# HGRN2 attention with a bilinear feed-forward: block 1 half in product triples, the weights' conversion in the list scheduler

## Chip, cores and metric

The kernel runs on one core of a Trainium2 chip. The metric is the device time of one execution in microseconds (us); the time of the kernel before is the median of three runs.

## What is computed

```
f = sigmoid(f_logit)                                   # (4 batches, 8 heads, 768 steps, 48)
state[t] = f[t][:, None] * state[t-1] + outer(k[t], v[t])
y[t]     = q[t] @ state[t]
x   = y of all heads side by side                      # 3072 tokens x 384
out = ((x @ w_a) * (x @ w_b)) @ w_out                  # w_a, w_b: 384 x 1536; w_out: 1536 x 384
```

All in float32 on the chip; the three weight matrices arrive as 64-bit floats.

## The kernel before

**Attention.** The scan is computed in 16 units of 2 x 2 heads and 384 steps, with running products of f (DVE scans), masked scores of 64 x 64 tokens, and states carried from chunk to chunk. Each unit needs loads of f, k, q and v (SP queue), a front on ACT, POOL and DVE (`front_parts`), matmuls (`core_parts`), and five stores of y into `xT` over SP (L554). Two units make the x of one block of 384 tokens; there are eight blocks.

**Feed-forward, up.** For a block, x @ w_b and x @ w_a are made in 12 column tiles of 128. In the direct form (`up_steps`, L598) a tile takes six matmuls of 384 columns, three into each of two PSUM banks. There are four banks, so a tile's two banks are those of the tile two before it. `product` (L618, L620) lets ACT copy the b half to SBUF and DVE multiply it with the a half; this frees the banks. Blocks 0 and 1 use the direct form for all 12 tiles. Blocks 2 to 7 use `up_triples` (L720): three column tiles k of a group j together, three row blocks of the weights and two halves of the tokens are multiplied with fifteen products instead of eighteen, from sums of weights (`combine_w_ba`) and sums of x (`combine_x`), 4 groups a block. The sums of weights overwrite parts of w_ba, so they can only be finished when no direct tile needs w_ba any more.

**Feed-forward, down.** `down` (L822) multiplies two token groups of 128 by w_out with seven products instead of eight, from sums of w_out (`combine_w_out`).

**Weights.** 20 pieces (`weight_pieces`: 14 of w_b and w_a by column tiles, 6 of w_out), 768 KB each (four are 384 KB), are loaded by SP (L258) and converted to float32 by `from_double` in steps: ACT makes the exponent word (L58) and the low word (L59), POOL bounds the exponent (L60), ACT makes the sign in two instructions (L62, L63), DVE shifts (L68) and adds (L73). A piece is loaded into one of four places of `raw`; pieces 4 and 5 lie in `groups`, where later the products of block 1 lie. Three pieces at a time have room for their intermediate words (`thirds`, `bits`).

**The order.** Every engine works through its instructions in the order in which the code emits them. Up to tile 5 of block 0 the order is written by hand. Then comes a loop over `ups`: block 0's tiles 6 and 7, then tiles of block 1 and block 0 in turn, and it converts the weights tile by tile as `needed` asks for them (`convert`, `begin`, `end`). The last tiles and all that follows are a list `main` of steps with costs; a list scheduler puts the steps of six `Line`s beside it (sums of w_out, sums of x, the attention's core and front, its loads, sums of w_ba). `fill` emits a line's step when by the planner's costs it can start within a beat (653 ns, one product on PE) and does not make a step of `main` late against its due beat, with a margin of 500 ns (`delays`). The sums of w_ba use 11 adding DMAs from the POOL queue (L630), six writes on ACT (L633) and four additions on DVE (L1256).

Of the kernel before, what the change touches and what calls it, by code (L numbers as in the profile page):

```python
# [12 lines left out]
FP32 = mybir.dt.float32  # L13
# [129 lines left out]
def by_quotients(ctx, tc, q, k, f_logit, v, moe_w_a, moe_w_b, moe_w_out, out, ident, weights, bad, ps_f):  # L143
# [53 lines left out]
    raw_places = itertools.cycle([raws4[:, PIECE * i:PIECE * i + PIECE] for i in range(4)])  # L197
# [43 lines left out]
    EARLY = (4, 5)  # L241
# [3 lines left out]
    def load_weights(n=1):  # L245
        for _ in range(n):
            if len(raws) == len(todo):
                return
            dst, src, (k, m) = todo[len(raws)]
            raw = dst  # L250
            if src.dtype != FP32:

                if len(raws) in EARLY:
                    raw = groups[:, EARLY.index(len(raws))].bitcast(mybir.dt.uint64)
                else:
                    raw = next(raw_places)
                raw = raw[:, 0:k * m].rearrange("p (k m) -> p k m", k=k)
            nc.sync.dma_start(out=raw, in_=src)  # L258
            raws.append(raw)
# [16 lines left out]
    def end(n):  # L276

        while ended[0] < min(n, len(todo)):
            begin(ended[0] + 1)
            next(going[ended[0]], None)  # L280
            ended[0] += 1
            if ended[0] > 2 and ended[0] - 1 not in EARLY:
                load_weights()

    def convert(n):
        while ended[0] < min(n, len(todo)):
            end(ended[0] + 1)
            begin(ended[0] + 2)
# [6 lines left out]
    firsts = groups[:, len(EARLY)].rearrange("p (u n s) -> p u n s", u=NQ, n=2)  # L295
# [6 lines left out]
    def front_parts(u):  # L302
# [38 lines left out]
        first = ((ACT, 930, opposite), (ACT, 750, sigmoid))  # L341
# [270 lines left out]
    def product():  # L612

        if not factors:
            return
        blk, ft, ps = factors.pop(0)
        b_sb = next(b_copies)
        nc.scalar.copy(b_sb, ps["b"][:, 0:BLK])  # L618
        a, b = (x.rearrange("p (g t) -> p g t", g=NTG) for x in (ps["a"][:, 0:BLK], b_sb))
        nc.vector.tensor_tensor(products(blk)[:, :, ft], a, b, ALU.mult)  # L620
        give_back(ps.values())
# [13 lines left out]
    def w_sums(steps, width):  # L635

        for to, x, what in steps:
            if what in (1, -1):
                yield ACT, width, 0, write, to, x, what
            elif what == "+":  # L640
                yield POOL, 1300, 0, add_by_dma, to, x
            else:
                yield DVE, width + 200, 0, nc.vector.tensor_tensor, to, x, *what
# [8 lines left out]
    def combine_w_out():  # L652
# [6 lines left out]
            (t1, b12, (b11, ALU.subtract)), (t2, b22, (t1, ALU.subtract)),  # L659
            (t4, b21, (t2, ALU.subtract)), (b12, b22, (b12, ALU.subtract)),  # L660
        ), 1070)

    def combine_w_ba():
# [10 lines left out]
        )  # L674
        return w_sums((
            (s[1], a12, 1), (s[4], a33, -1), (s[5], a11, -1), (s[1], a22, "+"), (s[4], a31, "+"), (s[5], a31, "+"),
            (s[3], a22, 1), (s[2], a12, 1), (s[0], a21, 1), (s[1], a23, "+"), (s[4], a21, "+"), (s[5], a32, "+"),
            (s[3], a23, "+"), (s[2], a22, "+"), (s[0], a32, "+"), (s[3], a32, "+"), (s[2], a21, "+"),
        ), 1000), w_sums((
            (a31, a11, (a31, ALU.subtract)), (a31, a31, (a33, ALU.add)),  # L680
            (a22, s[1], (a31, ALU.subtract)), (a22, a22, (a13, ALU.add)),
# [32 lines left out]
    def up_triples(blk):  # L714
# [28 lines left out]
        for j in range(NJ3):  # L743
# [9 lines left out]
            first, second = (x.rearrange("p (g n t) -> p g n t", g=2, n=2) for x in pairs)  # L753
# [15 lines left out]
            yield copy(3, first[:, :, 1], u)  # L769
# [3 lines left out]
            yield copy(3, first[:, :, 0], v)  # L773
            yield on(DVE, 870, 0, add_steps, c[:, :, 1:3, 1], c[:, :, 1:3, 1], first, copied=True)
# [5 lines left out]
            yield copy(3, second[:, :, 1], v)  # L780
# [5 lines left out]
            yield copy(2 if j == NJ3 - 1 else 3, second[:, :, 0], v)  # L786
            yield times(u, "u5", j)
            yield add(3, 2, 0, u)
            yield on(DVE, 870, 0, add_steps, c[:, :, 0], c[:, :, 0], second, copied=True)
# [178 lines left out]
    with tc.manual_schedule():  # L968
# [98 lines left out]
        end(3)  # L1067
        load_unit(3, "v")
        end(4)
        turn(2)  # L1070
# [21 lines left out]
        load_weights(2)  # L1092
# [6 lines left out]
        end(7)  # L1099
        mask(3)  # L1100
# [5 lines left out]
        end(8)  # L1106
        carried(3)
        product()
        begin(10)
        end(9)  # L1110
        up(0, 5)
# [5 lines left out]
        ups = [(0, 6), (0, 7)]  # L1117
        for i in range(8, NFT):
            ups += [(1, i - 8), (0, i)]
        ups += [(1, i) for i in range(NFT - 8, NFT)]  # L1120
        alone = len(todo) - 7
        for n, (blk, i) in enumerate(ups[0:alone]):
            convert(needed(i))
            up(blk, i)
            end(8 + n)
            product()
            begin(ended[0] + 2)
            if 2 < n < 2 + 2 * NSET and n % 2:
                load_unit(NSET + n // 2, "kqv" if n == 3 else "fkqv")


        w_out_sums, (w_before, w_over) = list(combine_w_out()), combine_w_ba()
        main, beside, behind, ending = [], {}, {}, []
        for blk, i in ups[alone:]:
            main.extend(up_steps(blk, i))
            main.append(on(DVE, 480, 2, product))
        behind[0] = behind[1] = len(main)
        ahead = 4
        for blk in range(NBLK):
            if blk >= 2:  # L1140
                beside[len(main)] = "x", blk
                main.extend(up_triples(blk))
# [4 lines left out]
            if blk == 1:  # L1147
                pairs = (((0, 1), (0, 2)), *pairs)
            for two in pairs if blk else ():
# [4 lines left out]
                beside = {n + (n > at): x for n, x in beside.items()}  # L1154
# [4 lines left out]
                behind.setdefault("down", len(main))  # L1159
# [15 lines left out]
        for_out, for_x, core, fore, loads, for_ba = lines = [Line() for _ in range(6)]  # L1175
        marks = {"out": for_out.extend(w_out_sums)}
        for_ba.extend(w_before)
        marks["ba"] = for_ba.extend(w_over, past=behind[1])
        stores = {}
        for s in range(2 * NQ, NU + 1):  # L1180
            if s < NU:
                loaded = ()
                if s - NSET in stores:
                    at = stores[s - NSET]
                    loaded = (loads.extend([(SP, ISSUE, 6000, do) for do in loads_of(s)], needs=(at,)),)
                ready = fore.extend(
                    [(e, load, 0, *do) for part in front_parts(s) for e, load, *do in part], needs=loaded
# [10 lines left out]
            if s > 2 * NQ and s % NQ == 0:  # L1198
                blk = s // NQ - 1
                one_by_one = combine_x(blk)  # L1200
                marks["x", blk] = for_x.extend(
                    [(e, load, 0, next, one_by_one) for e, load in X_STEPS],
                    needs=(stores[s - 1],),
                    past=behind[blk - 1] if blk > 2 else behind["down"],
                )

        LATENCY, MARGIN = 200, 500
        now, free_at, done = 0, [0] * 5, 0
# [11 lines left out]
        def delays(engine, start, load):  # L1220
# [17 lines left out]
            for ready, cost, due in later:  # L1238
# [3 lines left out]
                if with_it + MARGIN > max(starts.get(due, 1 << 30), without + MARGIN):  # L1242
# [3 lines left out]
        def emit(line, start):  # L1246
            nonlocal now
# [4 lines left out]
            else:  # L1252
                free_at[engine] = start + load
            line.ends.append(start + load + after)
# [11 lines left out]
        def fill():  # L1266
            more = True
            while more:
                more = False
                for line in lines:  # L1270
# [15 lines left out]
        for done, (engine, load, due, do, *args) in enumerate(main):  # L1286
            if done in beside:
                emit_until(*marks[beside[done]])
                if beside[done] == ("x", 2):
                    emit_until(*marks["ba"])  # L1290
# [363 lines left out]
```

## Time and profile before

| | |
|---|---|
| median of 3 runs | 596.82 us (596.09 to 597.02) |
| the profiled execution | 596.65 us |
| its span | 594.9 us |
| PE's granted clock, mean | 0.997 |
| direct matmuls L598, 128x384, 288 records | busy 95.6 us |
| adding DMAs L630, 11 | 8.5 us median to landing |
| ACT waits for PE's triples (sums, L1301) | 68.2 us |

The span runs from the first instruction to the last. PE is TensorE, DVE VectorE, ACT ScalarE, POOL GpSimd, SP SyncE, which only issues DMAs here. A float32 matmul leaves two records. The busy time of a group counts overlapping records once, so one product is priced by the distance of the next, not by its own duration. An engine's idle time is put down to the instruction that released it.

### The profile page before, as it was taken

Reading aid. Unit: us, or ns where it says so; the run is one execution under the profiler, and the core shown is the slowest. Engines: PE = TensorE matmul, PEld = TensorE weight load, DVE = VectorE, ACT = ScalarE, POOL = GpSimd, SP = SyncE. Lnnn points to the kernel's source line nnn. Section 1 sums busy time; section 2 is a strip of 40 time slices with the busy share of each in tenths; the row PEclk is TensorE's granted clock in tenths of the full one; section 3 lists DMA queues with packets and bytes.
Section 4 is the critical chain, followed back from the end, with each engine's and each line's share of the span. In section 5 each row is a group of like instructions: output and inputs, shape, how many; then the busy total and the mean of one; then the engine's idle time right before and its main releaser. Section 6 shows DMA issues by size and latency. Waiting matters only on the chain.

```text
span 594.9 us, 13948 instructions
## 1 busy us (share of the span) xinstructions
PE 573.2 (96%) x5802; PEld 513.2 (86%) x5802; DVE 411.9 (69%) x786; ACT 268.9 (45%) x507; POOL 77.6 (13%) x71
## 2 busy tenths in 40 slices
PE   3899999999999999999999999999999999999996
PEld 1655655567999999999999999999999999999996
DVE  6899445599978678958895678837785265745741
ACT  6589959743122464245521344326431335135300
POOL 6254525355000000000000000000000000000000
PEclk9899999999999999999999999999999999999999
DMA  8696698099552440043005400041001100000000
GB/s 205 192 261 211 220 264 257 0 154 186 115 141 66 115 99 4 15 120 95 2 1 127 115 15 1 2 112 36 3 1 47 48 1 0 2 28 1 0 29 33
DMA packets 33273, 49.43 MB, mean 83 GB/s; under 512 B 3952, under 2 KB 24976, under 8 KB 33200
## 3 DMA queue, kind: packets, MB, share of 16 engines
q1 hardware_dynamic: 30000, 42.38, 25.8%
q0 software_dynamic: 3056, 5.92, 5.8%
q8 instruction: 47, 0.77, 0.5%
q14 instruction: 26, 0.21, 0.1%
q10 hardware_dynamic: 144, 0.15, 0.1%
HBM read 33.23 MB, written 4.72 MB: 64 GB/s over the span
## 4 chain that ended last, share of the span: by engine, by line
PE 84%; DVE 11%; issue 2%; ACT 1%; DMA 1%; SPq 0%; DVEq 0%; ACTq 0%
PE ps_f L720 35%; PE ps_f L822 28%; PE ps_f L598 13%; PE ps_y L489 2%; DVE inv L335 2%; PE ps_y L515 2%; PE ps_x L392 2%; PE ps_x L440 1%; PE ps_x L416 1%; DVE sums L712 1%; DVE f_in L322 1%; DVE groups L712 1%; DVE st L469 1%; DVE q_in L339 1%; DVE spare L335 1%
## 5 line engine op out<-in xcount | busy, mean ns | idle before, releaser
L598 PE MATMUL ps_f<-xT,w_ba 128*128 128x384 f32 x288 | 95.6, 489 | 0.9 <-DMA xT<-y 0.7
L1301 ACT COPY sums<-ps_f 128x384 f32<-128x384 f32 x120 | 57.4, 480 | 75.9 <-PE ps_f L720 68.2
L598 PEld LDWEIGHTS ps_f<-xT,w_ba 128*128 128x128 f32 x288 | 54.0, 190 | 37.5 <-issue 1.6
L1301 ACT COPY groups<-ps_f 128x384 f32<-128x384 f32 x120 | 57.7, 481 | 62.9 <-PE ps_f L720 39.9
L720 PE MATMUL ps_f<-xT,w_ba 128*128 128x192 f32 x384 | 78.5, 327 | 0.0
L720 PEld LDWEIGHTS ps_f<-xT,w_ba 128*128 128x128 f32 x384 | 64.8, 190 | 0.2
L720 PE MATMUL ps_f<-groups,w_ba 128*128 128x192 f32 x288 | 55.5, 328 | 0.0
L720 PE MATMUL ps_f<-x_sums,raw 128*128 128x192 f32 x288 | 54.1, 331 | 1.2 <-DVE groups L712 0.9
L822 PE MATMUL ps_f<-w_out,sums 128*128 128x192 f32 x288 | 52.2, 329 | 0.3 <-DVE groups L620 0.3
L822 PE MATMUL ps_f<-w_out,groups 128*128 128x192 f32 x288 | 51.7, 329 | 0.0
L720 PEld LDWEIGHTS ps_f<-x_sums,raw 128*128 128x128 f32 x288 | 46.9, 190 | 4.3 <-DVE groups L712 1.8
L822 PE MATMUL ps_f<-spare,sums 128*128 128x192 f32 x288 | 49.0, 327 | 0.0
L720 PEld LDWEIGHTS ps_f<-groups,w_ba 128*128 128x128 f32 x288 | 47.9, 190 | 0.5 <-ACT groups L1301 0.3
L822 PEld LDWEIGHTS ps_f<-w_out,sums 128*128 128x128 f32 x288 | 47.1, 190 | 1.3 <-DVE groups L620 0.6
L318 POOL TENSOR_SCALAR inv<-inv 128x768 f32<-128x768 f32 x14 | 13.1, 934 | 266.4 <-ACT inv L315 266.3
L822 PEld LDWEIGHTS ps_f<-w_out,groups 128*128 128x128 f32 x288 | 47.1, 190 | 0.7
L822 PEld LDWEIGHTS ps_f<-spare,sums 128*128 128x128 f32 x288 | 47.1, 190 | 0.1
L60 POOL TENSOR_SCALAR sums<-sums 128x768 f32<-128x768 f32 (+1 forms) x20 | 40.4, 2018 | 44.5 <-ACT sums L58 44.5
L712 DVE TENSOR_TENSOR sums<-sums,groups 128x768 f32<-128x768 f32 x36 | 34.7, 964 | 14.2 <-ACT groups L1301 13.7
L712 DVE TENSOR_TENSOR sums<-ps_f,sums 128x384 f32<-128x384 f32 x60 | 32.8, 553 | 16.5 <-PE ps_f L720 15.1
L720 PE MATMUL ps_f<-x_sums,w_ba 128*128 128x192 f32 x192 | 39.4, 328 | 0.5 <-DVE sums L712 0.5
L720 PE MATMUL ps_f<-xT,raw 128*128 128x192 f32 x192 | 39.5, 328 | 0.0
(142 smaller groups left out, 870.3 us busy)
## 6 DMA issues: line engine op xcount, KB each, us to landing
raw<-w_ba POOLq DMA_DIRECT2D x11, 512.0 KB, 8.5
k_in<-in_k_dram SPq DMA_DIRECT2D x32, 144.0 KB, 3.7
q_in<-in_q_dram SPq DMA_DIRECT2D x32, 144.0 KB, 4.5
v_in<-in_v_dram SPq DMA_DIRECT2D x16, 288.0 KB, 5.6
raw<-in_moe_w_out_dram SPq DMA_DIRECT2D x6, 768.0 KB, 6.0
out_dram<-o SPq DMA_DIRECT2D x22, 192.0 KB, 1.9
f_in<-in_f_logit_dram SPq DMA_DIRECT2D x28, 144.0 KB, 3.1
xT<-y SPq DMA_DIRECT2D x45, 72.0 KB, 2.2
```

Of the source, the lines that this page charges most:

```text
L60: nc.gpsimd.tensor_scalar(h, h, HI_MAX, None, ALU.min)
L318: nc.gpsimd.tensor_scalar(inv, inv, EXP_K, 1.0, ALU.mult, ALU.add)
L322: nc.vector.tensor_tensor_scan(F[:, c], F[:, c], none, math.exp(MIDDLE), ALU.mult, ALU.add)
L335: nc.vector.tensor_tensor_scan(inv[:, w], inv[:, w], none[:, 0:C], first, ALU.mult, ALU.add)
L392: nc.tensor.matmul(ps[h][SUB * p:SUB * p + SUB, o:o + SUB], lhsT=kf[r, tokens(n, c, p)], rhs=qf[r, tokens(n, c, p)], start=True, stop=True,)
L489: nc.tensor.matmul(ps[p][e:e + D, o:o + SUB], lhsT=t["v"][r, n, c, h * D:h * D + D], rhs=at[r, h, o:o + SUB], start=o == 0, stop=True, ski ...
L515: nc.tensor.matmul(ps[p][e:e + D, o:o + SUB], lhsT=st[j][r, n], rhs=qf[r, tokens(n, c, p)], start=False, stop=True, skip_group_check=True,)
L598: nc.tensor.matmul(ps[nm][:, 0:BLK], lhsT=w[:, kt, ft * 128:ft * 128 + 128], rhs=xT[blk][:, kt], start=kt == 0, stop=kt == NKT - 1,)
L712: nc.vector.tensor_tensor(to, x, y, op)
L720: nc.tensor.matmul(ps[:, g], lhsT=sums_of_w[name][:, g, 128 * j:128 * j + 128], rhs=sums_of_x[blk][name], start=start and g == 0, stop=Tru ...
L822: nc.tensor.matmul(to, lhsT=x[:, i // 2, i % 2], rhs=w[:, NI * (i % 2) + i // 2], start=start and i == 0, stop=i == HFT - 1, skip_group_ch ...
L1301: do(*args)
```

## The change

- Block 0's tiles 6 to 11 come first, without tiles of block 1 between them. Then come six direct tiles of block 1 (groups j = 0 and 1), block 0's first `down`, and block 1's groups j = 2 and 3 as triples (`up_triples(1, first=2)`), which is 30 products in place of 36 direct matmuls.
- Pieces are loaded into six places, two of them in `groups`, in the order of `PLACES`. Four pieces are loaded at once after unit 2's y; the rest in the hand-written part follow the conversions.
- From piece 8 or so on, the conversion is three `Line`s of the list scheduler, as are the loads of weights and units. For six pieces (10, 11, 12, 13, 15, 17) the sign is one DVE instruction and not two on ACT.
- `product` is two steps of `main` with own due beats: ACT's copy, then DVE's multiplication. The margin is 1200 ns while the direct tiles last. The planner gives a weight piece 3200 ns, a unit's load 400 ns and 1500 ns more to land, and stops its own PE clock where a tile needs a piece.
- The sums of w_ba are 8 additions on DVE, two copies on ACT and four adding DMAs.

```diff
-    EARLY = (4, 5)
+    PLACES = (0, 1, 2, 3, 4, 5, 0, 1, 2, 3, 4, 5, 0, 1, 2, 3, 4, 5, 2, 3)
...
+    def piece_steps(i, sign_on_dve):
...
+        def sign_bits():
+            x = raws[i].bitcast(U16).rearrange("p k (n four) -> p (k n) four", four=4)[:, :, 3]
+            nc.vector.tensor_scalar(upper, x, 0x8000, None, ALU.bitwise_and)
...
+        yield ACT, 150 + n, 0, exponent
+        yield ACT, 240 + n, 0, rounded
+        yield POOL, 350 + 240 * n // 100, 0, bounded
+        if sign_on_dve:
+            yield DVE, 100 + n * 2 // 3, 0, sign_bits
+        else:
+            yield ACT, 300 + 220 * n // 100, 0, signs
...
         return w_sums((
-            (s[1], a12, 1), (s[4], a33, -1), (s[5], a11, -1), (s[1], a22, "+"), (s[4], a31, "+"), (s[5], a31, "+"),
-            (s[3], a22, 1), (s[2], a12, 1), (s[0], a21, 1), (s[1], a23, "+"), (s[4], a21, "+"), (s[5], a32, "+"),
-            (s[3], a23, "+"), (s[2], a22, "+"), (s[0], a32, "+"), (s[3], a32, "+"), (s[2], a21, "+"),
+            (s[1], a22, a23, add), (s[2], a12, a22, add), (s[2], a21), (s[0], a21, "copy"), (s[0], a32),
         ), 1000), w_sums((
-            (a31, a11, (a31, ALU.subtract)), (a31, a31, (a33, ALU.add)),
-            (a22, s[1], (a31, ALU.subtract)), (a22, a22, (a13, ALU.add)),
+            (s[3], s[1], "copy"), (s[4], a33, a31, less), (s[3], a32), (s[1], a12), (s[4], a21, s[4], less),
+        ), 1000), w_sums((
+            (a31, a11, a31, less), (s[5], a32, a31, less), (a31, a31, a33, add), (a22, s[1], a31, less), (a22, a22, a13, add),
         ), 950)
...
-    def up_triples(blk):
+    def up_triples(blk, first=0):
...
-        for j in range(NJ3):
+        for j in range(first, NJ3):
...
-        ups = [(0, 6), (0, 7)]
-        for i in range(8, NFT):
-            ups += [(1, i - 8), (0, i)]
-        ups += [(1, i) for i in range(NFT - 8, NFT)]
+        DIRECT = 2
+        SIGNS_ON_DVE = (10, 11, 12, 13, 15, 17)
+        ups = [(0, i) for i in range(6, NFT)] + [(1, j + NJ3 * k) for j in range(DIRECT) for k in range(NI)]
...
+            main.append(on(ACT, 480, 4, copy_factor))
+            main.append(on(DVE, 480, 6, multiply, copied=True))
...
+        loads, *conversions, for_out, for_ba, for_x, core, fore = lines = [Line() for _ in range(9)]
...
+                margin = 1200 if done < behind["direct"] else 500
+                if with_it + margin > max(starts.get(due, 1 << 30), without + margin):
...
+            if after < 0:
+                arrived = max(arrived, start) - after
+                after = arrived + 1500 - start - load
...
+                    if beside[done][0] == "w":
+                        now = max(now, line.ends[-1] + LATENCY)
```

## The prediction

> **What bounds the kernel now.** I read the page's busy time and slices first, then the chain of waits from 0 to 230 us, then the timelines of ACT and SP around 70 us, where the change acts.
>
> ```profile
> PE 573.2 (96%) x5802; PEld 513.2 (86%) x5802; DVE 411.9 (69%) x786; ACT 268.9 (45%) x507; POOL 77.6 (13%) x71
> ...
> PE   3899999999999999999999999999999999999996
> ...
> ACT  6589959743122464245521344326431335135300
> ```
>
> PE is full from the third slice on, ACT full only in slices 3 to 7. So after about 50 us the time is PE's work plus its gaps, and a gap can be made early, where ACT converts weights. The chain of waits (start, duration, what) says the same and prices PE's work:
>
> ```profile
> 66.30 62.13 PE ps_f L598 x192
> ...
> 210.05 11.91 PE ps_f L720 x72
> ```
>
> 192 records of the direct form without a gap are 16 column tiles (12 records each): 3.88 us a tile. L720 is the triples' line: 72 records are 18 products (4 each), 0.66 us; undisturbed ones in the timeline of PE follow each other by 0.65, which I take. PE's granted clock is 1.00 in this stretch, so it has nothing to give.
>
> **The gain.** One group of three column tiles costs 3 x 3.88 = 11.65 us direct and 15 x 0.65 = 9.75 in triples. Two groups of block 1 change over: 2 x 1.90 = **3.8 us less PE work**. In PE's queue of the changed kernel the 30 products stand there, so the change does what it says; the other PE work is the same, moved.
>
> **The price.** Before, tiles of block 1, which need only weights already there, alternate with those of block 0, and the last weight piece is finished at 115 us. Block 0 alone asks for the w_ba pieces twice as fast. These arrive in time: by the DVE queue summed with rows of before (shift 0.55, three adds of 0.35), piece 11 is finished at 77.5 and piece 13 at about 80, and PE needs them at 79.9 and 87.7. What is late is something else: the PSUM banks. A tile's first matmul waits for ACT's copy of the tile two before it, and ACT's queue now has loads to wait for ahead of these copies. Here is ACT before (start, duration, what, idle before):
>
> ```profile
> 72.50 0.88 ACT L58 ACTIVATE sums<-raw 128x768 f32<-128x768 f32 x1
> 73.27 1.00 ACT L59 ACTIVATE spare<-raw,whole 128x768 f32<-128x768 uint32 x1
> 74.17 0.87 ACT L62 ACTIVATE spare<-raw 128x768 bf16<-128x768 f32 x1
> 75.08 1.07 ACT L63 ACTIVATE spare<-spare 128x768 uint16<-128x768 bf16 x1
> 76.02 0.83 ACT L618 COPY x_sums<-ps_f 128x384 f32<-128x384 f32 x2
> 80.08 0.48 ACT L618 COPY x_sums<-ps_f 128x384 f32<-128x384 f32 x1 [3.24 <-PE ps_f L598]
> ```
>
> From start to start: exponent 0.80, low word 0.90, sign pair 0.93 + 0.94, copy 0.40; half pieces 0.45 and 0.53; a 1024-wide copy 0.95 (L633, three in 2.84). Before, ACT waits for PE (3.24 us at 80.08); in the changed order it is the other way round. Its queue from the copy of tile 5 at 67.88: exponent and low word of pieces 10 and 11 with tile 6's copy between, the same of half piece 12, two sigmoids (1.81), half piece 13, tile 7's copy: ends 76.25. Exponent 14 writes the buffer of piece 11, free at 77.5; with low word 14 and piece 15's two it ends at 80.95. Next stands exponent 16, and **behind it the copy of tile 8**. So piece 16's landing decides. SP before:
>
> ```profile
> 67.39 3.41 SPq L554 DMA_DIRECT2D xT<-y  x5
> 70.86 0.59 SPq L258 DMA_DIRECT2D raw<-in_moe_w_a_dram  x1
> 71.56 0.45 SPq L258 DMA_DIRECT2D raw<-in_moe_w_out_dram  x1
> 72.10 0.89 SPq L217 DMA_DIRECT2D k_in<-in_k_dram  x2
> 73.09 1.57 SPq L217 DMA_DIRECT2D q_in<-in_q_dram  x2
> 74.71 0.43 SPq L217 DMA_DIRECT2D v_in<-in_v_dram  x1
> 75.23 7.14 SPq L258 DMA_DIRECT2D raw<-in_moe_w_out_dram  x2
> ```
>
> In the changed queue pieces 8 to 14 go before the five xT stores, then 15 takes the place at 70.9, the five k, q, v loads follow, and 16 and 17 take the place at about 74.7, one 0.55 us issue earlier. The piece that stands there before took this long, and the DMA engines ran dry as the windows show (PE, PEld, DVE, ACT, POOL busy, clock, DMA share, GB/s):
>
> ```profile
> DMA to landing us min/median/max: 9.4/9.4/9.4
> ```
>
> ```profile
> 81.00:81.50 0.50, 0.50 (x4) 0.24 (x3) 0.00 (x0) 0.50 (x3) 0.41 (x1) 1.00 1.01 352
> 81.50:82.00 0.50, 0.50 (x3) 0.37 (x2) 0.00 (x0) 0.48 (x2) 0.50 (x1) 1.00 0.35 117
> ```
>
> Landing row: 74.7 + 9.4 = 84.1. Engines dry: 82. I take 84, the row of the same transfer in the same place; half piece 13 is no longer ahead (about 1 us at the 390 GB/s that weights reach), but 17 now follows at once. The Trainium skill (DMA: Bandwidth & Descriptors, Anatomy of one DMA) gives a fixed cost of about 2.0 us, mostly the receipt after the last byte. Here landing follows the end of traffic by 2.8; by the page's figure piece 16 would be there about a microsecond earlier, and the sum below 1 us less.
>
> From exponent 16's start, ACT's queue to the copies: tile 8's ends after 0.80 + 0.45 = 1.25; with sign pair 14, low word 16, exponent 17, tile 9's ends after 5.2; with sign pair 16, low word 17, exponent and low word 18, tile 10's after 10.1; with exponent and low word 19, a 1024-wide copy and sign pair 18, tile 11's after 15.0. PE without waits would start tile 10 at 81.8, 11 at 85.7, block 1's first tile at 89.6, its second at 93.5. With 84 as the start, tile 10 begins at 85.25 (3.4 late), 11 at 89.2 (0.1 more), the first of block 1 at 94.1 (1.0 more), the second at 99.0 (1.0 more): **5.5 us of PE idle**. After that two copies follow within 3 us and PE leads again.
>
> Bounds. Below: ACT never waits for a landing, starts exponent 16 at 80.95, and tile 11's copy ends at 96.0, 2.5 late. Above: piece 18. It is issued when sign 14 has read its buffer, at 86.1, and such pieces take 5.4 to 6.1 us in the timeline of SP's loads (91.5 to 92.2, in time by a hair); at 9.4 it lands at 95.5, and 7.1 us of ACT's queue stand between it and the end of tile 11's copy: 102.6, 9.1 late.
>
> **What costs nothing.** The sign bit on DVE is not in this trace; nearest are the shift of the same width (0.55 us) and the mask multiply (0.95): 0.5 to 1 us for each of six pieces, in a DVE queue that waits for ACT's copies there; it saves ACT 1.87 each, which is in the sums above. The seven adding DMAs that go (1.2 us of POOL each, 5.4 to 13.9 to land) free no PE: no matmul waits for them before. The four that stay could lengthen piece 18's landing, hence the upper end. w_out's pieces are done near 102, its sums (4 x 1.35) near 108, before the down stage at about 121. In that stage DVE has, from the last direct product, five w_ba sums of 1.13, three of 0.93 and two small ones to do, then x's first sums: about 12 us, beside 13.7 of PE (seven products of 1.95). If that cover fails, the triples start late by the excess, 0 to 2 us. PE's own gaps in that stretch before (0.30 and 0.75 between 138 and 150) may go or stay: -1.05 to 0. Later blocks keep their steps in a slightly other order; before, PE idles 1.7 us between 210 and 400, so -1 to +1; I take 0.
>
> **Sum.** The profiled execution took 596.65 us (span 594.9, 1.75 around it), 0.17 below the median 596.82. 596.65 - 3.8 + 5.5 = 598.35, say **598.4**, 0.26% above the median. With the median as base it would be 0.2 more.
>
> **Rivals.**
> 1. ACT is starved by piece 16 as worked out: 598.4. For it: the landing row and the place of tile 8's copy. Chance 0.45.
> 2. The landings are early enough, only ACT's own work holds PE up (2.5), and PE's old gap of 1.05 goes: 596.65 - 3.8 + 2.5 - 1.05 = 594.3, or 595.4 with the gap. It needs piece 16 by 81, against the windows, which show full engines until 81.5; for it is that a half piece less is queued. It decides the sign: faster if the idle stays below 2.6. Chance 0.27.
> 3. Piece 18 is late too, because a 512 KB adding DMA now runs beside it: 596.65 - 3.8 + 9.1 = 602.0. For it: the adds' landings up to 13.9. The skill (same page, SWDGE vs HWDGE vs iDMA) says that an engine alternates between software and hardware queues; no run here shows how much a load then loses. Chance 0.18.
> 4. The landings are as in 1, and DVE is not done when the triples start: 1 to 2 us more, 599.4 to 600.4. Chance 0.10.
>
> **How the numbers follow.** Slower by over 0.2% means above 598.0, faster below 595.6 (0.2% is about what a measurement of this kernel tells from no change). Case 1 spreads by its landing (82 gives 596.4, 85 gives 599.4): 0.27 slower, 0.18 same. Case 2: 0.22 faster, 0.05 same. Cases 3 and 4 are slower, but for 0.02 each, which I give to same and to faster. Together faster 0.24, same 0.25, slower 0.51. The range goes from case 2's low end, 594.3, to 602.3, just above case 3.
>
> **What would show it.** Right: PE gaps at tiles 10 and 11 of block 0 and at block 1's first two, ended by ACT copies; ACT idle before an exponent, ended by a w_out load landing near 84; 30 L766 products of block 1 without gaps; the PE work of the span lower by 3.8. Wrong: no gap over 1 us before 100 us (case 2); a long idle of ACT near 92, ended by piece 18 (case 3); PE waiting for DVE at the triples' first products (case 4).

## The result, and the profile after

The changed kernel takes **602.68 us** (median of 8 runs, 598.81 to 605.01) against 596.70 (596.09 to 597.36, 8 runs) for the kernel before on the same chip: ratio 1.0094, 95% interval 1.0079 to 1.0110. It is slower, on the side I forecast as likelier, but 0.4 us above the top of my range. The profiled execution took 602.55 us, its span 600.8.

The page's busy times and slices of the changed kernel:

```profile
PE 570.9 (95%) x5850; PEld 518.8 (86%) x5850; DVE 435.8 (73%) x818; ACT 262.1 (44%) x506; POOL 71.0 (12%) x64
...
PE   3789986999999999999999999999999999999996
...
DVE  6899698989987688948895776747775255836651
ACT  6589987213533345236532353326431245235300
```

PE works 2.3 us less and yet the kernel is 6 us longer. The new hole is the 6 in PE's seventh slice, 90 to 105 us. The timeline of PE there (start, duration, what, and in brackets the idle time before it and what ended it) shows four gaps, 6.87 us in all, where the kernel before had none:

```profile
84.04 4.14 PE L640 MATMUL ps_f<-xT,w_ba 128*128 128x384 f32 x12 [1.33 <-ACT x_sums L661]
89.13 4.14 PE L640 MATMUL ps_f<-xT,w_ba 128*128 128x384 f32 x12 [0.95 <-ACT x_sums L661]
93.94 4.14 PE L640 MATMUL ps_f<-xT,w_ba 128*128 128x384 f32 x12 [0.68 <-ACT x_sums L661]
101.99 15.38 PE L640 MATMUL ps_f<-xT,w_ba 128*128 128x384 f32 x42 [3.91 <-ACT x_sums L661]
```

They stand ahead of block 0's tiles 10 and 11 and block 1's first and second tile, and each is ended by the PSUM copy of a tile (L661, L618 before). ACT's timeline shows what was ahead of the first two copies, and the wait ahead of the fourth:

```profile
79.23 0.94 ACT L302 ACTIVATE sums<-raw 128x768 f32<-128x768 f32 x1 [1.81 <-DVE w_ba L322]
80.06 0.99 ACT L305 ACTIVATE spare<-raw,whole 128x768 f32<-128x768 uint32 x1
80.95 0.92 ACT L302 ACTIVATE sums<-raw 128x768 f32<-128x768 f32 x1
81.75 1.03 ACT L305 ACTIVATE spare<-raw,whole 128x768 f32<-128x768 uint32 x1
82.72 0.90 ACT L302 ACTIVATE sums<-groups 128x768 f32<-128x768 f32 x1
83.53 0.46 ACT L661 COPY x_sums<-ps_f 128x384 f32<-128x384 f32 x1
...
87.78 0.93 ACT L302 ACTIVATE sums<-groups 128x768 f32<-128x768 f32 x1 [1.01 <-DVE w_out L322]
88.59 0.48 ACT L661 COPY x_sums<-ps_f 128x384 f32<-128x384 f32 x1
...
97.02 0.93 ACT L302 ACTIVATE sums<-raw 128x768 f32<-128x768 f32 x1 [3.12 <-DMA raw<-in_moe_w_out_dram]
```

Exponents 14 (79.23) and 17 (87.78) wait for DVE's last pass over piece 11 and piece 14, whose buffers they take. Exponent 16 (82.72) shows no wait: piece 16, issued at 75.67 and 7.0 us under way, landed at about the moment ACT came to it. For the fourth gap I read the chain of waits, from 87 us on:

```profile
87.68 1.22 DVE spare L316
88.92 8.02 DMA raw<-in_moe_w_out_dram
96.97 0.04 issue
97.02 0.93 ACT sums L302
97.94 0.87 ACT spare L305
98.81 0.94 ACT raw L1346
99.74 0.79 ACT spare L311
100.56 1.06 ACT spare L312
101.62 0.33 ACT x_sums L661
101.94 0.04 issue
101.99 15.38 PE ps_f L640 x42
```

DVE makes the sign bits of piece 15 at 87.68, which frees raw place 3; only then SP issues piece 19, which lands after 8.0 us; exponent 19 stands in ACT's queue, and tile 11's copy behind it. The last line holds one more loss: 42 records take 15.38 us, and 13.81 in runs without it (below). The windows (busy PE, PEld, DVE, ACT, POOL; clock; DMA share; GB/s) show PE's clock falling to half for some three microseconds after the gap:

```profile
100.00:102.00 2.00, 0.01 (x1) 0.01 (x1) 0.03 (x1) 1.97 (x4) 1.52 (x2) 0.94 0.01 4
102.00:104.00 2.00, 2.00 (x3) 1.16 (x4) 1.97 (x4) 1.97 (x3) 0.00 (x0) 0.50 1.08 187
104.00:106.00 2.00, 2.00 (x6) 1.14 (x5) 1.97 (x4) 1.31 (x3) 0.60 (x1) 0.71 0.44 75
```

What I expected to be free of waits was so: down and triples follow each other without a gap until 162 us (PE's timeline):

```profile
137.30 2.11 PE L868 MATMUL ps_f<-w_out,sums 128*128 128x192 f32 x12
139.25 0.81 PE L766 MATMUL ps_f<-x_sums,raw 128*128 128x192 f32 x4
139.90 0.81 PE L766 MATMUL ps_f<-x_sums,w_ba 128*128 128x192 f32 x4
...
162.21 1.57 PE L766 MATMUL ps_f<-x_sums,raw 128*128 128x192 f32 x8 [0.63 <-DVE groups L758]
```

### The profile page after: what moved, and what is told of

It reads as the page before. It is cut to its first block, busy times and chain, and to the rows that moved or that the text cites. A ratio compares the mean times of both kernels' runs of the same rounds, so it can differ in the third digit from the quotient of the medians.

```text
span 600.8 us, 14055 instructions
## 1 busy us (share of the span) xinstructions
PE 570.9 (95%) x5850; PEld 518.8 (86%) x5850; DVE 435.8 (73%) x818; ACT 262.1 (44%) x506; POOL 71.0 (12%) x64
## 4 chain that ended last, share of the span: by engine, by line
PE 79%; DVE 10%; ACT 4%; DMA 4%; issue 3%; SPq 0%; DVEq 0%; ACTq 0%
PE ps_f L766 40%; PE ps_f L868 28%; PE ps_f L640 4%; PE ps_y L531 2%; DMA raw<-in_moe_w_b_dram 2%; PE ps_x L434 1%; PE ps_y L557 1%; DMA raw<-in_moe_w_out_dram 1%; PE ps_x L482 1%; PE ps_x L458 1%; DVE groups L758 1%; DVE inv L377 1%; DVE spare L377 1%; ACT y L576 1%; ACT sums L302 1%
## 5 line engine op out<-in xcount | busy, mean ns | idle before, releaser
L1392 ACT COPY sums<-ps_f 128x384 f32<-128x384 f32 x130 | 62.2, 481 | 84.1 <-PE ps_f L766 73.2
L1392 ACT COPY groups<-ps_f 128x384 f32<-128x384 f32 x130 | 62.5, 481 | 66.0 <-PE ps_f L766 42.2
L766 PE MATMUL ps_f<-xT,w_ba 128*128 128x192 f32 x416 | 85.3, 328 | 0.0
L640 PE MATMUL ps_f<-xT,w_ba 128*128 128x384 f32 x216 | 75.0, 500 | 8.5 <-ACT x_sums L661 6.9
L640 PEld LDWEIGHTS ps_f<-xT,w_ba 128*128 128x128 f32 x216 | 40.7, 194 | 37.8 <-ACT x_sums L661 9.3
L766 PEld LDWEIGHTS ps_f<-xT,w_ba 128*128 128x128 f32 x416 | 70.0, 190 | 0.8 <-ACT groups L1392 0.5
L766 PE MATMUL ps_f<-x_sums,raw 128*128 128x192 f32 x312 | 58.2, 331 | 2.3 <-DVE groups L758 2.2
L766 PE MATMUL ps_f<-groups,w_ba 128*128 128x192 f32 x312 | 60.4, 328 | 0.0
L766 PEld LDWEIGHTS ps_f<-x_sums,raw 128*128 128x128 f32 x312 | 51.0, 190 | 5.7 <-DVE groups L758 4.1
L766 PEld LDWEIGHTS ps_f<-groups,w_ba 128*128 128x128 f32 x312 | 51.9, 190 | 0.5 <-ACT sums L1392 0.2
L758 DVE TENSOR_TENSOR groups<-ps_f,groups 128x384 f32<-128x384 f32 x65 | 34.5, 550 | 6.3 <-PE ps_f L766 6.0
```

The lines of the kernel that those rows point to most:

```text
L640: nc.tensor.matmul(ps[nm][:, 0:BLK], lhsT=w[:, kt, ft * 128:ft * 128 + 128], rhs=xT[blk][:, kt], start=kt == 0, stop=kt == NKT - 1,)
L758: nc.vector.tensor_tensor(to, x, y, op)
L766: nc.tensor.matmul(ps[:, g], lhsT=sums_of_w[name][:, g, 128 * j:128 * j + 128], rhs=sums_of_x[blk][name], start=start and g == 0, stop=Tru ...
L1392: do(*args)
```

## The experiments

Every kernel is the changed one with the edit shown. Times are medians; gaps, waits and landings are those of one profiled execution each; the ratio is to the kernel before on the same chip, with its 95% interval. Gaps are PE's, from 66 to 128 us, in order. In the expectations, ACT's "exponent" and "low word" are L302 and L305.

**Piece 19 issued earlier (e1).**

```diff
-                raw = raw_place(PLACES[len(raws)])
+                raw = raw_place(6 if len(raws) == 19 else PLACES[len(raws)])
```

> Only the buffer of weight piece 19 is changed: it loads into a place of its own (the third of the groups tile) and no longer into raw place 3, so its issue does not wait for DVE's sign bits of piece 15. Theory A (the late landing of piece 19 makes the 3.9 us gap of PE before block 1's second tile, and the lower clock after the gap follows from the gap): piece 19 is issued right behind piece 18 near 85.5 us, lands at 91 to 94 instead of 97, its exponent waits for no load, the gap falls from 3.9 to under 1 us, the clock of the window 102 to 110 is back above 0.97, and the time falls by 3 to 5.6 us, to 597 to 599.7. Rival B (the adding DMA and the q, k, v loads beside it hold the landing back, not the issue): the landing stays at 95 or later, the gap at 2 us or more, the time above 600.5. Rival C (the clock loss has nothing to do with the gap): the gap goes, the window's clock stays near 0.8, the time falls by 3 or less.

603.18 us, 1.0080 (1.0059 to 1.0101); gaps 1.20, 0.95, 1.76, 3.46. Piece 19 was issued 3.4 us earlier and did not land earlier at all; the chain of waits:

```profile
85.49 11.89 DMA groups<-in_moe_w_out_dram
```

So the issue is not the cause: theory A fell, rival B held. The DMA engines are full here (busy share 0.95 from 66 to 100 us in the changed kernel), and the load that was issued earlier was under way longer.

**Piece 19 behind the copy (e2).** Emission is unchanged, but the first three steps of piece 19 are kept in a list until tile 11's copy stands in the queue.

```diff
+        if i == 19:
+            steps = [partial(waiting.append, x) for x in steps]
...
+        if factors[0][0:2] == (0, 11):
+            for x in waiting:
+                x()
```

> Landing and issue of piece 19 stay as they are; only its first three steps (exponent and low word on ACT, the bound on POOL) are put behind the PSUM copy of block 0's last column tile in ACT's queue. Theory A (the copy is late only because exponent 19 stands ahead of it and waits for the load): the copy runs near 98 instead of 101.5, the gap before block 1's second tile is 0 to 0.8 us, the clock stays above 0.97, the time falls by 3 to 5.6 us, to 597 to 599.7, although piece 19 still lands near 97. Rival B (what follows on PE waits for something else that is late as well, w_out's last piece or DVE): the gap moves to a later place with at least 2 us, the time stays above 600.5.

600.65 us, 1.0057 (1.0038 to 1.0076); gaps 1.06, 0.96, 0.71, 0.26, and a new one. PE's timeline:

```profile
98.91 11.88 PE L643 MATMUL ps_f<-xT,w_ba 128*128 128x384 f32 x36 [0.26 <-DVE groups L672]
...
112.89 1.03 PE L437 MATMUL ps_x<-q_in,k_in 48*64 48x64 f32 x48 [2.11 <-DVE q_in L384]
```

Both theories were half right. The order of ACT's queue made the fourth gap, and taking it away brings a wait for DVE 14 us later, which the late copies had hidden, with a clock of 0.79 in the eight microseconds from 110.

**The first adding DMA later (e3).**

```diff
-        nc.gpsimd.dma_start(out=to, in_=x, accum_op=ALU.add)
+        adds.append((to, x))
+        if len(adds) == 1:
+            return
+        for to, x in adds[0:2] if len(adds) == 2 else adds[-1:]:
+            nc.gpsimd.dma_start(out=to, in_=x, accum_op=ALU.add)
```

> The first of the four adding DMAs, which ran beside the loads of pieces 18 and 19, is held back and issued together with the second. Theory A (the issue of piece 19 waits for DVE's sign bits of piece 15): piece 19 is still issued near 88.9 and lands at 95.5 to 97, the gap stays at 3 us or more and the time within 1.5 us of the changed kernel's 602.7. Rival B (the adding DMA takes the bandwidth from the load): the load takes 5 to 6 us instead of 8, lands at 94 to 95, the gap falls to under 2 us, and the time to 599 to 600.5.

600.95 us, 1.0061 (1.0047 to 1.0075); gaps 1.44, 1.08, 0.69, 1.87, 0.75, and no drop of the clock. Piece 19, issued at 88.4, landed at 94.9, 2.0 us earlier than in the changed kernel: 0.5 of it by its issue, 1.5 by a shorter time under way (6.5 us for 8.0). That is close to rival B: the adding DMA holds the load back, as my third rival had it, for another piece.

**Signs 14 and 16 on DVE (e4).**

```diff
         def signs():
+            if i in (14, 16):
+                return sign_bits()
```

> The signs of pieces 14 and 16 are made by DVE in one operation (as for six other pieces) instead of by two operations of ACT, 1.87 us each. Theory A (the first three gaps of PE, 1.3 + 0.95 + 0.7 us, come from the length of ACT's own queue between the copies; the fourth from the landing of piece 19): the gaps at tile 11 and at block 1's first tile go (1.6 us less), the first one stays (it lies ahead of the pairs taken away) or grows by what DVE has more to do, the fourth stays or grows, since piece 19 lands no earlier: 600.5 to 602.5. Rival B (all gaps are ACT's own work): all four shrink, together by 3 us or more, and the time falls under 599.5. Rival C (DVE is full there, and two more operations of 0.8 to 1.2 us delay the sign of 15 and with it piece 19): the fourth gap grows by 1 to 2 us, and the time is at or above 602.7.

603.34 us, 1.0108 (1.0084 to 1.0131); gaps 1.02, 1.42, 1.21, 2.99, 0.75. ACT's queue is 3.7 us shorter, and two of the small gaps grow. Rival B fell; so did theory A's account of the small gaps, for they do not come from ACT's work alone. ACT's exponents 14, 17, 18 and 19 now wait 1.94, 3.38, 2.26 and 2.19 us for DVE (in the changed kernel 1.81 and 1.01 for 14 and 17). That is rival C's reason, and its time held too, but the fourth gap shrank where it had it grow.

**Unit 6's loads behind exponent 19 (e5), and the adding DMA too (e6).** In e5 they are issued from ACT's queue; e6 adds e3's edit.

```diff
-            nc.sync.dma_start(out=to, in_=src)
+            (nc.scalar if u == 6 else nc.sync).dma_start(out=to, in_=src)
...
+            if u == 6:
+                loaded[u] = (loads.extend([(ACT, 60, 2000, do) for do in loads_of(u, names)], (read[19],)),)
+                return
```

> The seven loads of unit 6 (1,152 KB), which SP issued from 89 to 92 us right behind piece 19, are issued from ACT's queue after exponent 19 instead; the first adding DMA stays. Theory A (the 16 DMA engines are full there and serve everything that is queued in turn, so that piece 19 lands late whenever it is issued): without 1.15 MB at some 300 GB/s beside it, piece 19 lands 2 to 3.6 us earlier than in the changed kernel, at 93.5 to 95, and the gap before block 1's second tile is 0.5 to 2 us. Rival B (one queue serves in order, so that loads behind piece 19 cost it nothing and only the adding DMA, on another queue, does): piece 19 lands at 96.5 to 97.5 as before and the gap stays at 3 us or more.

> Both are taken away from beside piece 19: unit 6's loads (as in the run above) and the first adding DMA (held back to the second one's place). Its issue still waits for DVE's sign bits of piece 15, near 88.9. Theory A (full DMA engines): piece 19 then has the engines with only the end of piece 18 beside it, lands 5 us or less after its issue, at 92.5 to 94, and the fourth gap is under 0.7 us; the first three gaps stay, together 2.5 to 3.5 us; time 597.5 to 600. Rival B (a landing of 8 us is what such a load takes in that place, whatever runs beside it): lands at 96 or later, gap 2 us or more.

e5: 602.72 us, 1.0090 (1.0073 to 1.0107); landing at 95.8, gaps 1.15, 0.96, 1.55, 2.64, and the clock at 0.83 after them. Piece 19 landed 1.1 us earlier, but 0.7 of that is its earlier issue (88.24 for 88.92); it was under way 7.6 us for 8.0. So the loads queued behind it cost it 0.4 to 1.1 us, the adding DMA (e3) 1.5 to 2.0: between A and B. e6: 599.43 us, 1.0039 (1.0029 to 1.0050); landing at 94.7, later than I expected, gaps 1.57, 1.08, 0.71, 1.18, 0.80, clock 1.00 throughout. Both together bring 3.2 us; the small gaps stay.

**All copies first, by the scheduler (e7).** The first step of pieces 14 to 19 may not be emitted before a given copy is.

```diff
-                read[i] = line.extend(steps[:4], needs)
+                behind_copy = {14: 8, 15: 8, 16: 9, 17: 10, 18: 11}
+                past = copy_at[0, behind_copy[i]] if i in behind_copy else copy_at[1, 0] if i == 19 else 0
+                read[i] = line.extend(steps[:4], needs, past)
```

> The order of ACT's queue alone: the first step of a w_out piece is not put into the queue before the PSUM copy of a certain tile stands there (pieces 14 and 15 behind the copy of block 0's tile 8, 16 behind 9, 17 behind 10, 18 behind 11, 19 behind that of block 1's first tile). Loads and adding DMAs are as full as before. Theory A (all four gaps of PE come from copies that stand behind conversions of pieces which PE needs only 25 us later): all four gaps go, together under 1 us left instead of 6.9, no drop of the clock there; the w_out sums end 2 to 5 us later, still before the down stage; time 602.7 - 6 to 8.5, so 594.2 to 596.7, at or below the kernel before. Rival B (DVE is the bound of that stretch, and what is put off comes back as a wait of PE for DVE or for w_out between 110 and 140): as much as 3 to 7 us returns there, time 598 to 602.

605.31 us, 1.0134 (1.0117 to 1.0150). The four gaps go; one of 1.01 us is left in the middle of tile 11, ended by DVE. But the scheduler filled the room with the attention of the next unit, and PE ran into it:

```profile
100.66 1.66 PE L434 MATMUL ps_x<-q_in,k_in 48*64 48x64 f32 x48 [7.38 <-DVE q_in L381]
```

Rival B held in kind, earlier than it had it (100 us) and larger than its own figure. The test was not clean, since PE's order changed too.

**The copies first, in ACT's queue alone (e8), and with e6's edits (e9).** As in e2, for pieces 16 to 19; DVE and PE keep their order. A sign operation of a piece first puts out what is still kept of that piece and those before it.

```diff
+    def flush(i=19):
+        while waiting and waiting[0][0] <= i:
+            waiting.pop(0)[1]()
...
+        if i > 15:
+            steps = [partial(waiting.append, (i, x)) for x in steps]
...
         nc.scalar.copy(factors[0][3], factors[0][2]["b"][:, 0:BLK])
+        flush()
```

> Pieces 16 to 19: in ACT's queue their exponent (with low word, and the bound on POOL, where these come early) stands behind the next PSUM copy of a column tile instead of ahead of it. DVE's and PE's order is untouched, DMAs too. Theory A (the four gaps are copies standing behind these exponents): the first three gaps fall from 3.0 to under 1.2 us together, the fourth to under 0.5; PE reaches block 1's second tile 5 to 6 us earlier. What then comes: theory A1 (nothing else is late) gives 602.7 - 6 to 8 = 594.7 to 596.7. Rival A2 (DVE, 95% busy there, is as late as ACT): the lead comes back as one wait of PE near 108 to 113 for DVE's products of q and k, 2.1 us where only piece 19 was put off, here 3 to 5 us; with a clock drop behind it the time is 598 to 600.5. Rival B (the gaps stay): 602 to 603.

> Both remedies: unit 6's loads behind exponent 19, the first adding DMA held back, and the copies ahead of the exponents of pieces 16 to 19. If DVE is the bound behind the copies (rival A2 of the run before), the order brings at most 1.5 us beyond the 599.4 of the traffic alone: 598 to 599.5. If not (A1), all four gaps go and nothing returns: 595 to 597.

e8: 601.85 us, 1.0082 (1.0054 to 1.0110). PE's timeline:

```profile
82.09 9.96 PE L649 MATMUL ps_f<-xT,w_ba 128*128 128x384 f32 x30 [0.26 <-ACT x_sums L670]
93.55 2.20 PE L649 MATMUL ps_f<-xT,w_ba 128*128 128x384 f32 x6 [1.50 <-DVE groups L676]
97.62 14.03 PE L649 MATMUL ps_f<-xT,w_ba 128*128 128x384 f32 x42 [1.86 <-ACT x_sums L670]
...
113.87 1.42 PE L443 MATMUL ps_x<-q_in,k_in 48*64 48x64 f32 x48 [2.23 <-DVE q_in L390]
```

The copies of tiles 8 to 10 are early now, and two of the four waits are ended by DVE: rival A2, with more left over than it had. The wait of 1.86 us, ahead of block 1's second tile, is another matter. Tile 11's copy still stands behind exponent 18, and that waited for piece 18, which was under way 8.3 us here:

```profile
92.60 0.89 ACT L306 ACTIVATE sums<-raw 128x768 f32<-128x768 f32 x1 [2.21 <-DMA raw<-in_moe_w_out_dram]
```

e9: 600.04 us, 1.0042 (1.0026 to 1.0059); gaps 0.23, 0.47, 2.39, 0.58, then the clock at 0.64 from 98 to 102. On top of e6 the order brings nothing.

**One group more or less in triples, on e6 (e10, e11).** `DIRECT = 3` and `DIRECT = 1`.

> The kernel without the traffic, with three instead of two groups of block 1 direct: one group is taken back from the triples. The gain's size: if it is 1.9 us a group, as worked out from 3 x 3.88 - 15 x 0.65, and free of gaps, this is 599.4 + 1.9 = 601.3 (600.8 to 601.8). If half of it is eaten by waits at the triples, 600.4 or less. DVE and weight sums have 11.6 us more until the triples start, so no new wait.

> The same, with one group direct: one more group in triples. If nothing is late, 599.4 - 1.9 = 597.5. But the direct tiles end 11.6 us earlier, and the sums of w_ba and of x that the triples need have so much less time: DVE, which had them done without a wait to spare that the trace shows, is then late, by 3 to 9 us, and the time is 600 to 607. I hold the second for likelier, 3 to 1.

e10: 599.71 us, 1.0042 (1.0025 to 1.0059), that is 0.3 over e6 and not 1.9. PE's waits behind 140 us are 1.2 us here and 2.7 in e6, and the gaps ahead of 128 are 4.31 and 5.34: what the second group saves PE in work, it spends in waits. (The profiled execution of e10 was its slowest, with a clock of 0.50 from 52 to 54 us, so only the waits are compared.) e11: 604.00 us, 1.0123 (1.0106 to 1.0140). PE waits 2.58 us for DVE's last sums of w_ba at 130 us: late, as I held likelier.

**Work put off to after the sums of w_out (e12), and everything together (e13).** e13 adds e5's edit and e8's order, with the signs of 18 and 19 behind the copy as well.

```diff
-            if i == 13:
-                for_ba.extend(w_early, pieces())
...
-        for_ba.extend(w_late, pieces())
+        for_ba.extend(w_early, (*pieces(), marks["out"][0]))
+        for_ba.extend(w_late)
```

> The two early sums of w_ba (DVE, 2.6 us), ACT's wide copy and all four adding DMAs are moved behind the sums of w_out; nothing else is asked of the scheduler. Theory A (DVE, ACT and the DMA engines are all full from 78 to 100 us, so only taking work out of that stretch helps, not reordering it): the gaps of 66 to 128 us fall from 6.9 to 3.5-5 us and the time to 599 to 600.5; DVE has room for the sums between 118 and 139, where it idled 3 us. Rival B (the sums are needed: they come too late for the triples): PE waits 2 us or more for w_ba between 125 and 145, time 601 or more. Rival C (the early sums were free): gaps and time as in the changed kernel, 602 to 603.

> Everything at once: the early sums and adding DMAs behind w_out's sums, unit 6's loads behind exponent 19, the copies ahead of the exponents of pieces 16 to 19 and of the signs of 18 and 19. Theory A: gaps of 66 to 128 us under 2.5 us in all, no drop of the clock, time 602.7 - 4.4 - 1.5 = 596.8, within 1 (595.8 to 597.8), so about the kernel before. Rival D (the wait only moves on, to DVE's products of q and k near 112 and to the triples near 125 to 160): 598.5 to 600.5.

e12: 607.13 us, 1.0163 (1.0130 to 1.0196); e13: 602.91 us, 1.0099 (1.0078 to 1.0120). In e12 the gaps up to 128 us are 1.04, 1.49, 0.73 and 3.10, nearly those of the changed kernel, as rival C had it. At the fourth, exponent 19 waits only 1.15 us for its load, but ACT's sign operations of pieces 18 and 19 now both stand ahead of tile 11's copy. In e13 the gaps are 0.49, 1.36 and 1.91. In both runs the sums are late for the triples. PE's timeline of e12:

```profile
148.82 0.92 PE L766 MATMUL ps_f<-xT,w_ba 128*128 128x192 f32 x4 [2.58 <-DVE w_ba L1345]
```

So theory A fell, and rivals B and D held in kind, with e13's time above D's figure: work that is put off comes back as a wait at the triples.

**4 us of DVE's work left out, on e8 (e14) and on e13 (e15).**

```diff
-            (t1, b12, b11, ALU.subtract), (t2, b22, t1, ALU.subtract),
-            (t4, b21, t2, ALU.subtract), (b12, b22, b12, ALU.subtract),
-        ), 1070)
+        return w_sums(tuple((*(x[:, :, 0:48] for x in y), ALU.subtract) for y in (
+            (t1, b12, b11), (t2, b22, t1), (t4, b21, t2), (b12, b22, b12),
+        )), 1070)
```

> The order of the run e8 (copies ahead of the exponents of pieces 16 to 19), and DVE's four sums of w_out done for 48 of every 192 columns, so that about 4 us of DVE's work near 100 to 108 us are left out (the rest of the columns is left as it was, so the output is not the reference's). Theory A (DVE's queue is the bound behind ACT's): the wait for DVE's products of q and k near 112 us, 2.2 us in e8, goes and with it the drop of the clock behind it, the gaps ahead of 100 us stay; time 601.85 - 2.2 - 1.5 = 598.2 (597 to 599.5). Rival B (that wait has another cause, such as unit 5's loads): it stays, time 601 or more.

> The run e13 (everything at once), with the same 4 us of DVE's work left out. There DVE stood idle for 3 us only between 76 and 140 us, and PE waited for it four times (1.4 and 1.9 us near 100 and 105, 2.6 us near 146, and once more through ACT's copies). Theory A (DVE is the bound of the whole stretch up to the triples): every wait behind 105 us shortens, together by about the 4 us left out; time 598 to 600. Rival B (the waits near 146 have their own cause, the adding DMAs that come late): they stay; time 601.5 or more.

e14: **597.39 us**, 1.0003 (0.9992 to 1.0014), in theory A's range. The waits at 98 and 114 us of e8 are gone, the one near 93 is 0.6 longer; this is all that PE's timeline has left between 92 and 128:

```profile
93.64 17.39 PE L649 MATMUL ps_f<-xT,w_ba 128*128 128x384 f32 x48 [2.10 <-DVE groups L676]
```

The time is 4.5 us below e8's with 3.6 us less work on DVE, but not all of it is that work. The wait near 114 (2.23 us) and the slow clock behind it are what theory A named. The wait at 98 (1.86 us) came before the work left out, which starts at 101.6 us; it is missing because piece 18 was under way 6.0 us here and not 8.3, so exponent 18 did not wait. Theory A had the gaps ahead of 100 us stay. e15: 603.43 us, 1.0104 (1.0074 to 1.0134), no gain: rival B's figure. The wait of 2.59 us for w_ba near 147 stays. Rival B's reason, late adding DMAs, is not in the chain of waits: DVE works without a pause from 140.71 to 146.92, first sums of x, then four sums of w_ba. Five of these sums may only be emitted behind the last direct tile; that they stand too far back in the queue is read from its order, no run moved them. So near 114 us DVE's work is shown to be what PE waits for behind ACT's copies. No run here has all waits gone with the whole work done, and none beats the kernel before.

## Why the prediction was right or wrong

**The gain: right.** PE's busy time fell from 573.2 to 570.9, and 1.57 of the latter is the slow clock (15.38 against 13.81 for 42 records): 3.9 us less work, 3.8 forecast. But e10 shows that the second group's share of it does not reach the time.

**The mechanism: right, its sizes not.** PSUM copies behind exponents in ACT's queue hold PE up at exactly the four tiles named, and e2 and e8 take gaps away by that order alone. But 3.4, 0.1, 1.0 and 1.0 us were forecast and 1.33, 0.95, 0.68 and 3.91 measured: that the sums, 5.5 and 6.87, are not further apart is luck.

**The step that failed: "tile 11's after 15.0".** Tile 11's copy was to end 15.0 us after the start of exponent 16. It ended after 19.2 (82.72 to 101.94). ACT's own work was priced rightly; the difference is two waits that the sum put at nothing, 1.01 us of exponent 17 for DVE and 3.12 of exponent 19 for the landing of piece 19. I had landings for pieces 16 and 18 and none for 19, which took 8.0 us beside an adding DMA and unit 6's loads. With both of them moved away the kernel is 3.2 us faster (e6). The clock that fell behind this gap and the late front, both below, make up the rest.

**"So piece 16's landing decides": not so as worked out.** Piece 16 was there at about 82.7, not at 84, just when ACT came to its exponent (82.72). ACT was no earlier because exponent 14 had waited 1.81 us for DVE's last pass over piece 11, and started at 79.23 and not at 77.5. So the load and DVE held exponent 16 up alike. That is not my second rival, which wanted the piece by 81 and counted ACT's work alone: of its 2.5 us 1.45 lie in the first three gaps (10.1 after 80.95, against 89.6), where 2.96 were measured. Piece 18 was in time. The third rival had the right partner, the adding DMA, at the wrong load, and e3 shows what a load loses to it; that its 602.0 is near the measured time is luck. The skill's fixed cost of 2.0 us, which I set beside the landing, is the page's fit for DMAs that GpSimd issues; piece 16 is issued by SP.

**"What costs nothing": it cost something.** I gave the sign bits "0.5 to 1 us for each of six pieces, in a DVE queue that waits for ACT's copies there", and no cost. Their size was right, 0.83 us each. But I never added up DVE's queue between 66 and 118 us. The windows of the kernel before, then of the changed one (third pair: DVE):

```profile
66.00:118.00 52.00, 52.00 (x185) 30.74 (x174) 23.50 (x47) 42.54 (x62) 20.79 (x11) 1.00 0.58 168
```

```profile
66.00:118.00 52.00, 45.13 (x222) 25.77 (x222) 44.13 (x70) 36.21 (x52) 30.14 (x17) 0.97 0.80 210
```

DVE was busy 23.5 of 52 us and is busy 44.1, in a stretch in which the DMA engines went from 58% to 80%. The groups of DVE in the same stretch of the changed kernel (busy, mean ns of one, idle before) show what came:

```profile
L322 DVE CUSTOM_DVE_ANT_0 w_out<-sums,spare 128x1536 uint16<-128x1536 uint16 x6 | 6.7, 1120 | 0.4
...
L1346 DVE TENSOR_TENSOR raw<-w_ba 128x1024 f32<-128x1024 f32 x3 | 3.7, 1218 | 0.0
L1346 DVE TENSOR_TENSOR spare<-w_out,spare 128x1152 f32<-128x1152 f32 x2 | 2.7, 1352 | 0.0
L316 DVE TENSOR_SCALAR spare<-raw 128x384 uint16<-128x384 uint16 (+1 forms) x3 | 2.6, 868 | 0.0
L364 DVE TENSOR_TENSOR_SCAN f_in<-f_in,zero 128x384 f32<-128x384 f32 x2 | 2.5, 1263 | 0.0
L316 DVE TENSOR_SCALAR spare<-groups 128x768 uint16<-128x768 uint16 x3 | 2.4, 790 | 0.0
```

Sign bits 5.0 us; sums of w_ba 3.7 (there are nine additions on DVE in all, not eight as written above); sums of w_out, most of which fell behind 118 before (1.3 of 5.4 us ahead of it), 5.5; the next unit's scans and products. All of it has a place in a queue, and through buffers ACT's exponents, the issue of piece 19 and PE's attention wait for it. With "the other PE work is the same, moved" I had moved PE's work; DVE's moved with it. What the runs show of its price is ACT's waits of 1.81 and 1.01 us for DVE in the changed kernel, and the 2.1 to 2.2 us that PE waits for DVE near 113 us once the copies are early (e2, e8); the latter go when DVE has 3.6 us less to do (e14).

**"PE's granted clock is 1.00 in this stretch, so it has nothing to give": it had something to lose.** 1.57 us in the profiled run. This term was missing.

**The rest.** Tile 6 started at 66.96 us and not at 66.23, so tile 10, without its gap, would have started at 82.7. In the other runs with this order of the front that figure is 81.3 to 83.1 (e10 and e13, whose clock fell between 34 and 56 us, left out), so the 0.7 is scatter. The sum 598.35, plus 1.37 for gaps, 1.57 for the clock and 0.73 for the front, is 602.0 of the 602.55 measured; half a microsecond is not assigned.

## What to carry to other kernels

Before an edit on an idle-looking engine is costed at nothing, add up that engine's busy time up to the next deadline, with all that moves into the stretch: a queue that is 85% busy passes on every wait that is taken off its neighbour. Where the DMA engines are full, count the bytes beside a load and not its issue time, and give every load that a queue waits for a landing, the last one too. And a gap of PE of more than two microseconds may be followed by a slow clock, so price it with a surcharge (1.6 to 3.1 us here).

## What the runs showed of the hardware

**The clock after a gap.** Where the windows of 2 or 4 us show PE's clock at 0.50 to 0.7, the same 42 direct records take 15.4 to 16.9 us and not 13.81. It fell after gaps of 2.10 (e14), 2.11 (e2), 2.23 (e8), 2.27 (e15), 2.39 (e9), 2.58 and 3.10 (e12), 2.64 (e5), 3.46 (e1), 3.91 (the changed kernel) and 7.38 us (e7), and not after 1.87 (e3), 2.58 (e11, e13), 2.59 (e15) or 2.99 (e4). In e1 it stayed low for more than six microseconds:

```profile
102.00:104.00 2.00, 1.56 (x3) 0.96 (x4) 1.55 (x3) 1.97 (x4) 0.00 (x0) 0.50 0.84 147
104.00:106.00 2.00, 2.00 (x5) 1.09 (x4) 2.00 (x4) 1.54 (x3) 0.16 (x1) 0.50 0.68 115
106.00:108.00 2.00, 2.00 (x5) 1.09 (x4) 1.93 (x3) 0.48 (x1) 2.00 (x2) 0.50 0.23 41
```

The Trainium skill (TensorE: Matmul & The Clock Gate, Part 1: The HAM clock gate) describes half speed after an idle window of about 3.4 us that runs freely, and full speed again after about 3.4 us of work. The half speed agrees. That gaps of 2.1 us are enough, the page does not say, and a window that must be idle throughout would not explain them; why a gap of 2.99 is spared and one of 2.10 is not stays open. This may be why the changed kernel scatters over 6 us where the kernel before scatters over 1.3; that was not tested.

**An earlier issue that lands no earlier** (e1): 11.9 us under way for 768 KB, against 8.0 when issued 3.4 us later.

**DVE's passes are longer in the fuller stretch.** The last pass over a w_out piece takes 0.96 us each time before; after, 0.96 or 1.44 to 1.46, 1.12 in the mean, and POOL's bound of a piece takes 2.5 in the mean instead of 2.2. They overlap more often now; that this is the cause was not tried.
